# Clearing two tiles on VectorE at the start, and twelve extra matmuls ahead of the first transposes

## The chip, the cores and the metric

The kernel runs on one core of a Trainium2 chip. The core has engines that each work through their own queue of instructions in order: TensorE (PE in the profile; its weight loads are listed as PEld), VectorE (DVE), ScalarE (ACT), GpSimd (POOL) and SyncE (SP), which here does nothing but issue transfers. The metric is the time of one execution on the device in microseconds; lower is better. Engines wait for each other by semaphores; the waits that appear in the profile are inferred from these.

## The reference

A forward pass of a small speech model and all its gradients, in bf16:

```python
h = gelu(conv3(x, w1))[:, ::2, :]          # B=2, T=16000, D=256
f = gelu(conv3(h, w2))[:, ::2, :]          # 4000 rows left per batch
fe = einsum("btd,de->bte", f, w_f)
ge = einsum("bud,de->bue", g, w_g)         # U=8 rows per batch
j = tanh(fe[:, :, None, :] + ge[:, None, :, :])
out = einsum("btud,dv->btuv", j, w_o)      # 2 x 4000 x 8 x 256
```

The kernel returns `out` and the gradients with respect to x, w1, w2, g, w_f, w_g and w_o for a given `grad_out`, eight outputs in all.

## The kernel before

The 8000 rows of f (both batches after each other) are cut into chunks: one of 256 rows, then chunks of 512, then a rest. For each chunk three stages follow each other, and the stages of neighbouring chunks overlap: `stage_a` (L542) computes the two convolutions with their gelu and gelu derivative, and fe as the tile FE; `stage_j` (L636) computes the joint tanh, the output, and the gradients that go back through the tanh; `stage_de` (L813) takes the gradient back through the convolutions.

`stage_j` goes through u in four pairs. For each pair ScalarE makes the tile JT (L654): tanh(FE + ge), with channels on the partitions and ge as a bias from the tile GE. The gradient of w_o needs the same values with rows on the partitions, JR. The first two chunks get JR from JT by transposes on TensorE into a PSUM tile `psb` (L681), which VectorE or ScalarE copies out. All later chunks (except the last) compute it anew: VectorE adds FER, the rows of fe, and GEB, and ScalarE takes the tanh (L686, L691).

GEB is ge for one batch, spread over all 128 partitions: 8 x 256 values in every partition. `make_geb` (L606) makes it from GER, ge as rows: it clears the whole tile (L609), copies the ge rows into partitions 0, 32, 64 and 96 with four transfers issued by POOL, and, much later, spreads these within each 32 partitions by a VectorE shuffle (L615). Two such tiles are made, one for each batch. `ge_rows` (L626) computes GER with matmuls on gT and WG (transposed g and the weight w_g); `make_ge` (L1071) computes gT and GE.

The order of the instructions on each engine is not the order of the program text. Every piece of work is an operation with an engine, an estimated cost, its dependencies and a due time (`F.now` or `at`). `Flow.issue` (L107) simulates the engines with these estimates: it always takes the operation that can start first, then the one with the earlier due time, and emits it. What comes out is a fixed order for each engine's queue. Due times count in rows of f: 0 is the start of the first chunk's `stage_j`; `BIG` is -1e9 and so comes first. Dependencies given to an operation only steer this simulation; a real wait is set by the framework below where instructions touch the same tile.

The buffers come from classes with fixed numbers of slots. The class `ps` has seven PSUM banks, given to whichever operation needs one next; `geb` has two slots, one for each GEB tile.

Before the first chunk there is a head: VectorE clears a small tile (L1043), TensorE does twenty matmuls on it that nobody reads (`warm_up`, L1048), ScalarE does a first activation, POOL makes the identity, and the loads of x, the weights and g go out on the queues of SP, ACT and POOL. `mm` (L336) is the helper of nearly all matmuls, so that most of them carry its line, L337. `dma` (L357) is the helper of all transfers.

Of the kernel before, what the change touches and what calls it, by code (L numbers as in the profile page):

```python
# [10 lines left out]
BF16 = mybir.dt.bfloat16  # L11
# [25 lines left out]
class Flow:  # L37
# [24 lines left out]
    def buf(self, cls, shape, dtype, name):  # L62
        b = Buf(cls, shape, dtype, name)
        s = self.seq[cls]
        b.seq, s[0] = s[0], s[0] + 1
        return b

    def op(self, eng, cost, fn, r=(), w=(), new=(), at=None, work=0.0, after=(), kind=None, behind=(), sub=None, lag=0.0):
        o = Op()
        o.eng = (eng,) if isinstance(eng, str) else tuple(eng)  # L70
        o.cost = cost if isinstance(cost, tuple) else (cost,) * len(o.eng)
        o.fn, o.new, o.work, o.n = fn, list(new), work, len(self.ops)
        o.prio = ((self.now if at is None else at) + self.shift.get((self.stage, sub), 0.0), o.n)
        o.succ, o.done, o.ready, o.kind, o.span, o.lag = [], None, 0.0, kind, None, lag
        deps, bufs = set(after), []
        for lst, wr in ((r, False), (w, True)):
            for x in lst:
                b, key = x if isinstance(x, tuple) else (x, None)
                for d, k, dw in b.log:
                    if (wr or dw) and (k is None or key is None or k == key):  # L80
                        deps.add(d)
                if b not in bufs:
                    bufs.append(b)
        for lst, wr in ((r, False), (w, True)):
            for x in lst:
                b, key = x if isinstance(x, tuple) else (x, None)
                if wr:
                    b.log = [e for e in b.log if not (key is None or e[1] == key)]
                b.log.append((o, key, wr))
        for b in o.new:  # L90
            b.born = o
        deps.discard(o)
        o.soft = ({b.born for b in bufs if b.born is not None} | set(behind)) - deps - {o}
        deps |= o.soft
        for b in o.new:
            if b not in bufs:
                bufs.append(b)
        o.deps, o.bufs = deps, bufs
        for b in bufs:
            b.users += 1  # L100
        o.left = len(deps)
        for d in deps:
            d.succ.append(o)
        self.ops.append(o)
        return o
# [102 lines left out]
def c_pe(ns):  # L208
    return sum(max(n / 2.4 + 2.5, 25.0) for n in ns)
# [6 lines left out]
def c_dve(n, f=1.0):  # L216
    return 66.0 + 1.042 * n * f
# [3 lines left out]
def kernel(  # L221
# [19 lines left out]
    nc = tc.nc  # L241
    B, T, D = x.shape
    KK = w1.shape[0]
    U = g.shape[1]
# [6 lines left out]
    P = 128  # L251
# [42 lines left out]
    F = Flow(ctx, tc)  # L294
    op, buf = F.op, F.buf
# [9 lines left out]
    def fixed(shape, dtype, name, pool=None):  # L305
        b = Buf(None, shape, dtype, name)
        b.t = (pool or const).tile(shape, dtype, name=name)
        return b

    def psum(dt=FP32):  # L310
        return buf("ps", [P, CW if dt == FP32 else 2 * CW], dt, "ps" if dt == FP32 else "psb")
# [5 lines left out]
    WG = fixed([P, KT, D], BF16, "WG")  # L317
# [5 lines left out]
    GER = fixed([U, B, D], BF16, "GER")  # L323
# [6 lines left out]
    GE = fixed([P, B, KT, U], FP32, "GE")  # L330
# [5 lines left out]
    def mm(ps_ap, lhsT, rhs, start, stop):  # L336
        nc.tensor.matmul(ps_ap, lhsT=lhsT, rhs=rhs, start=start, stop=stop)  # L337
# [19 lines left out]
    def dma(q, out, in_, r, w, bytes_, new=(), transpose=False, at=None, after=(), cost=None, behind=(), sub="dma"):  # L357
        def go(e):
            eng_ = nc.sync if e == "SP" else nc.gpsimd if e == "POOL" else nc.scalar
            if transpose:  # L360
                eng_.dma_start_transpose(out=out(), in_=in_())
            else:
                eng_.dma_start(out=out(), in_=in_())
        c = cost or (1230.0 if transpose else 750.0 if q == "POOL" else 450.0)
        return op(q, c, go, r=r, w=w, new=new, at=at, after=after, behind=behind, sub=sub, kind="T" if transpose else "D",
                  work=bytes_ / 32768 * 165.0 if transpose else bytes_ / 304.0)
# [74 lines left out]
    def load_got(k, up, at):  # L441
        c = chunks[k]
        A, Pw = c.A, c.Pw
        GO = st[k]["GO"][up]
        GOT = buf("got", [P, NB, 2, KT, P], BF16, "GOT")
        if c.last:
            dma("SP", lambda: GOT[:].rearrange("p a u k c -> p (a u k) c")[:, 0:UP * KT, 0:2 * Pw],
                lambda: GO[:2 * Pw].rearrange("p a u v -> p (a u v)")[:, 0:UP * V], r=[GO], w=[GOT],
                bytes_=Pw * U * V * 2, new=[GOT], transpose=True, at=at)
            st[k]["GOT"] = {up: GOT for up in range(UP)}  # L450
            return
        dma("SP", lambda: GOT[:, 0:A, :, :, :Pw].rearrange("p a u k c -> p (a u k) c"),
            lambda: GO[:Pw, 0:A].rearrange("p a u v -> p (a u v)"), r=[GO], w=[GOT],
            bytes_=Pw * A * 1024, new=[GOT], transpose=True, at=at, sub="got")
        st[k].setdefault("GOT", {})[up] = GOT
# [149 lines left out]

    def make_geb(b):  # L606

        GEB = buf("geb", [P, U, D], BF16, "GEB")
        op("POOL", 2100.0, lambda e: nc.gpsimd.memset(GEB[:], 0.0), r=[(GER, b)], w=[GEB], new=[GEB])  # L609
        for q in range(0, P, 32):  # L610
            dma("POOL", lambda q=q: GEB[q:q + 1], lambda: GER[:, b, :], r=[(GER, b)], w=[(GEB, q)], bytes_=4096)

        def spread(e):
            v = GEB[:].rearrange("p u d -> p (u d)").bitcast(FP32)
            nc.vector.stream_shuffle(v, v, [0] * 32)  # L615
        op("DVE", 66.0 + c_dve(U * D // 2), spread, r=[GEB], w=[GEB], sub="geb", lag=45000.0 if b == 0 else 100000.0)
        return GEB

    def mix_geb(G0, G1):
        px = [c.px for c in chunks if c.px is not None][0]  # L620
        GEB = buf("gx", [P, U, D], BF16, "GEB")
        op("DVE", c_dve(U * D, 0.25), lambda e: nc.vector.tensor_copy(out=GEB[:], in_=G1[:]), r=[G1], w=[GEB], new=[GEB])
# [378 lines left out]
    def gg_out():  # L1001
# [43 lines left out]
       r=[(warm, 0)], w=[(warm, 1)])  # L1045
# [4 lines left out]
            mm(wps[:, 0:2 * P], warm[:, 0, 0], warm[:, 0].rearrange("p k c -> p (k c)"), True, True)  # L1050
    op("PE", 20 * 215.0, warm_up, r=[(warm, 0)], w=[wps], new=[wps])
    op("POOL", 500.0, lambda e: make_identity(nc, ident[:]), w=[ident])

    def wload(q, dst, out, in_, n, at, after=()):
        return dma(q, out, in_, r=[], w=[dst], bytes_=n * 65536, at=at, cost=450.0 if q != "POOL" else 550.0, after=after)
# [41 lines left out]
    def part(k):  # L1097
        return str(k) if k < 4 else "e" if k >= NG - 2 else "s"

    W0 = float(chunks[0].W)  # L1100
    stage_a(0, -W0, W0)
    F.now = -0.3 * W0
    make_ge()
    GEB = GEBX = None
    for k in range(NG + 1):
        c = chunks[min(k, NG - 1)]
        t0, Wk = (c.t0, float(c.W)) if k < NG else (float(NP), 300.0)
        if k < NG:
            F.stage = part(k)
            for up in range(1 if c.last else UP):  # L1110
                load_go(k, up, t0 + Wk * (up / UP - 0.7), [xh] if k == 0 else [])
                load_got(k, up, t0 + Wk * (up / UP - 0.5))
        F.stage = part(k)
        if k + 1 < NG:
            load_xc(k + 1, t0 - Wk * 0.3, [st[0]["GOT"][1].log[0][0]] if k == 0 else [])
        if k == 0:
            fr = st[1]["XCl"]
            wt(WFT, w_f[:, :], 1, W0 * 0.6, [fr])
            wt(W2T, w2.rearrange("i k n -> (i k) n"), KK, W0 * 0.7, [fr])
            wt(W1T, w1.rearrange("i k n -> (i k) n"), KK, W0 * 0.8, [fr])  # L1120
        if k + 1 < NG and chunks[k + 1].px is not None:
            F.now = t0 + Wk * 0.3
            GEB1 = make_geb(1)
            GEBX = mix_geb(GEB, GEB1)
        if k == 1:
            F.now = t0 + Wk * 0.1
            ge_rows()
            GEB = make_geb(0)
        if k < NG:
            F.stage = "j" + part(k)  # L1130
            stage_j(k, t0, Wk, GEBX if c.px is not None else GEB)
        if k < NG and c.px is not None:
            GEB = GEB1
        if k + 1 < NG:
            F.stage = "a" + part(k)
            stage_a(k + 1, t0, Wk)
        if k >= 1:
            F.stage = "d" + part(k)
            stage_de(k - 1, t0, Wk)
        F.stage = None  # L1140
        if k == NG - 1:
            F.now = t0 + Wk
            gg_out()
# [33 lines left out]
```

## Time and profile before

| | |
|---|---|
| runs, us | 789.6, 791.91, 789.79 |
| median, us | 789.79 |
| profiled execution, us | 789.48 |
| its span, first to last instruction, us | 787.7 |
| mean granted TensorE clock | 0.995 of full speed |
| two POOL clears of GEB | 11.88 to 15.42 us |
| first tanh of JT | 17.33 us |
| first transposes of JT | 17.88 us |
| second chunk's first convolution | 28.95 us |
| shuffles of GEB | 78.7 and 147.5 us |

All positions are microseconds from the start of the span. The page of the profile lists each engine's busy time and share of the span, then the span in 40 slices with the busy share of each in tenths, and the clock that TensorE was granted. The timeline lists instructions in order of their start, equal ones merged: start, length, engine, line, operation, tiles, shape, count, and in brackets how long the engine had been idle before and what ended that. The windows list, for a stretch, each engine's busy time and count of instructions, then the granted clock, the share of transfer engines in use, and GB/s. In groups "128x512 bf16" is partitions by elements.

### The profile page before, as it was taken

The numbers are of one execution on the slowest core, as the hardware profiler recorded it, in microseconds if no ns is written. First come the engines' busy times: TensorE is split into PE (matmuls) and PEld (weight loads), VectorE is DVE, ScalarE is ACT, GpSimd is POOL, SyncE is SP. The second block draws the span as 40 slices with busy tenths as digits, with TensorE's granted clock in tenths as the row PEclk, the third lists the DMA queues.
The fourth block names the chain that finished last, engine by engine and source line by source line (L and its number), as shares of the span: only waits on it lengthen the run. The fifth ranks groups of instructions, "written<-read, shape, count | busy, mean of one in ns | idle before, by whom it ended". The sixth has DMA issues, their size and how long they took to land. (4 is left out here: it accounts for less than half of the span.)

```text
span 787.7 us, 15636 instructions
## 1 busy us (share of the span) xinstructions
PE 770.0 (98%) x5668; PEld 533.6 (68%) x5668; DVE 714.1 (91%) x1503; ACT 725.5 (92%) x1178; POOL 96.2 (12%) x235
## 2 busy tenths in 40 slices
PE   6999999999999999999999999999999999999997
PEld 4657767576675767767677666676767767577775
DVE  5799999998998989989899898998989899899965
ACT  4999989999999999999999999999999999999833
POOL 4311110201102010020101101010020110203010
PEclk8999999999999999999999999999999999999999
DMA  9998999999999999999999999999998989989984
GB/s 212 175 208 187 232 252 244 238 240 243 222 227 227 266 232 215 233 257 225 229 211 244 243 230 226 214 257 219 229 252 203 264 209 227 248 225 239 229 204 144
DMA packets 382754, 178.86 MB, mean 227 GB/s; under 512 B 307762, under 2 KB 376468, under 8 KB 380756
## 3 DMA queue, kind: packets, MB, share of 16 engines
q1 hardware_dynamic: 381122, 176.90, 100.2%
q8 instruction: 44, 0.72, 0.4%
q10 hardware_dynamic: 1138, 0.66, 0.3%
q0 software_dynamic: 416, 0.30, 0.1%
q14 instruction: 34, 0.28, 0.1%
HBM read 51.42 MB, written 50.34 MB: 129 GB/s over the span
## 5 line engine op out<-in xcount | busy, mean ns | idle before, releaser
L654 ACT ACTIVATE JT<-FE,GE 128x512 bf16<-128x512 bf16 (+4 forms) x288 | 185.2, 691 | 0.1
L739 DVE SCALAR_TENSOR_TENSOR NGZ<-JSQ,ps 128x512 f32<-128x512 bf16 (+3 forms) x252 | 149.9, 608 | 3.5 <-PE ps L337 3.2
L337 PE MATMUL ps<-WO,JT 128*128 128x256 bf16 x1000 | 149.1, 273 | 0.0
L337 PE MATMUL ps<-GOT,WOT 128*128 128x512 bf16 (+2 forms) x544 | 147.2, 363 | 0.1
L346 ACT CAST OUT_SB<-ps 128x512 bf16<-128x512 f32 (+1 forms) x215 | 129.0, 604 | 11.8 <-PE ps L337 11.7
L337 PEld LDWEIGHTS <-JT 128*128 128x128 bf16 x1000 | 97.7, 98 | 54.7 <-issue 0.2
L726 ACT ACTIVATE JSQ<-JT 128x1024 bf16<-128x1024 bf16 (+2 forms) x129 | 130.0, 1008 | 4.5 <-DVE NGZ L739 4.2
L337 PE MATMUL GWO<-GO,JR 128*128 128x256 bf16 x1000 | 130.0, 273 | 1.5 <-ACT JR L691 0.8
L691 ACT ACTIVATE JR<-JR 128x1024 bf16<-128x1024 bf16 x112 | 120.3, 1076 | 8.4 <-DVE JR L686 8.1
L756 DVE TENSOR_TENSOR ZS<-ZS,NGZ 128x1024 f32<-128x1024 f32 (+2 forms) x102 | 115.3, 1131 | 0.4
L337 PEld LDWEIGHTS <-JR 128*128 128x128 bf16 x1000 | 97.5, 98 | 17.8 <-ACT JR L691 1.5
L520 DVE SCALAR_TENSOR_TENSOR g_s<-g_sq,ps 128x512 bf16<-128x512 bf16 (+2 forms) x102 | 64.8, 638 | 39.9 <-ACT HTo L517 31.4
L337 PEld LDWEIGHTS <-W 128*128 128x128 bf16 x612 | 57.9, 98 | 59.9 <-issue 2.8
L337 PE MATMUL ps<-XC,W 128*128 128x512 bf16 (+2 forms) x408 | 84.5, 362 | 1.4 <-DMA XC<-in_x_dram 1.4
L337 PEld LDWEIGHTS <-X 128*128 128x128 bf16 (+1 forms) x756 | 73.8, 98 | 9.6
L686 DVE TENSOR_TENSOR JR<-FER,GEB 128x1024 bf16<-128x1024 bf16 x112 | 77.6, 697 | 1.5 <-PE GWO L337 1.0
L809 DVE TENSOR_TENSOR ACC<-ACC,ps 128x512 f32<-128x512 f32 x90 | 59.1, 679 | 18.1 <-PE ps L337 18.1
L337 PEld LDWEIGHTS <-WOT 128*128 128x128 bf16 x544 | 51.7, 98 | 21.6 <-issue 0.9
L348 ACT ACTIVATE GX_SB<-ps 128x512 bf16<-128x512 f32 (+1 forms) x107 | 63.3, 619 | 2.1 <-PE ps L337 1.8
L379 POOL COPY GF<-GF 128x254 bf16<-128x254 bf16 (+1 forms) x17 | 7.4, 435 | 469.4 <-issue 313.6
L514 ACT ACTIVATE g_sq<-ps 128x512 bf16<-128x512 f32 (+2 forms) x102 | 60.7, 595 | 1.0 <-PE ps L337 0.6
L337 PE MATMUL ps<-W1T,GHo 128*128 128x512 bf16 (+1 forms) x252 | 61.3, 326 | 0.0
(144 smaller groups left out, 1171.3 us busy)
## 6 DMA issues: line engine op xcount, KB each, us to landing
GO<-in_grad_out_dram SPq DMA_DIRECT2D x60, 512.0 KB, 5.5
out_dram<-OUT_SB SPq DMA_DIRECT2D x60, 512.0 KB, 6.7
X<-in_x_dram SPq DMA_DIRECT2D x15, 1088.0 KB, 7.1
out_dram<-GX_SB SPq DMA_DIRECT2D x30, 512.0 KB, 3.5
GOT<-GO SPq DMA_TRANSPOSE x65, 5.0
GO<-in_grad_out_dram SPq DMA_DIRECT2D x4, 256.0 KB, 4.8
out_dram<-OUT_SB SPq DMA_DIRECT2D x4, 256.0 KB, 3.6
XC<-in_x_dram SPq DMA_TRANSPOSE x62, 4.9
```

Source lines behind the costliest of these rows:

```text
L337: nc.tensor.matmul(ps_ap, lhsT=lhsT, rhs=rhs, start=start, stop=stop)
L346: nc.scalar.copy(out=dst(), in_=src())
L348: nc.scalar.activation(out=dst(), in_=src(), func=ACT.Copy, scale=scale)
L514: op("ACT", c_act(W, True), lambda e, mt=mt, ps=ps: nc.scalar.activation(out=sq[:, 0:A, mt, :Pw], in_=fl(ps[:, :W], A), func=ACT.Square, s ...
L520: op("DVE", c_dve(W), lambda e, mt=mt, ps=ps: nc.vector.scalar_tensor_tensor(out=s[:, 0:A, mt, :Pw], in0=sq[:, 0:A, mt, :Pw], scalar=1.0, ...
L654: nc.scalar.activation(out=fl(jtw(JT, j)[:, mt], A)[:, :, lo:hi], in_=FE[:, 0:A, mt, lo:hi], func=ACT.Tanh, bias=GE[:, b, mt, 2 * up + j:2 ...
L686: op("DVE", c_dve(n * 2 * D, 0.5), lambda e, lo=lo, n=n, m=m, JR=JR: nc.vector.tensor_tensor(out=JR[:m, 0:n], in0=S["FER"][:m, lo:lo + n]. ...
L691: op("ACT", c_act(n * 2 * D), lambda e, n=n, m=m, JR=JR: nc.scalar.activation(out=JR[:m, 0:n], in_=JR[:m, 0:n], func=ACT.Tanh), r=[JR], w= ...
L726: nc.scalar.activation(out=JSQ[:, :, :W], in_=jtw(JT, j), func=ACT.Square)
L739: nc.vector.scalar_tensor_tensor(out=fl(zap(), A)[:, :, lo:hi], in0=fl(JSQ[:, d2, :W], A)[:, :, lo:hi], scalar=1.0, in1=fl(ps[:, :W], A)[: ...
L756: nc.vector.tensor_tensor(out=a, in0=a, in1=b, op=ALU.add)
L809: op("DVE", c_dve(512), lambda e: nc.vector.tensor_tensor(out=acc_ap().rearrange("p k d -> p (k d)"), in0=acc_ap().rearrange("p k d -> p ( ...
```

## The change

Three edits. `make_geb` no longer allocates and clears its tile; it takes one of two tiles that are made beforehand. These two are allocated in the head and cleared there by VectorE, written as 32-bit words, at the earliest due time, behind the clear of the small tile. And after `make_ge`, with a due time shortly before the first chunk's `stage_j`, TensorE gets twelve matmuls on WG (128 x 128 weights, 256 columns) into a PSUM bank that nobody reads. In the planner they depend on the second GE copy; the instructions themselves read only WG.

```diff
@@ make_geb @@
     def make_geb(b):
 
-        GEB = buf("geb", [P, U, D], BF16, "GEB")
-        op("POOL", 2100.0, lambda e: nc.gpsimd.memset(GEB[:], 0.0), r=[(GER, b)], w=[GEB], new=[GEB])
+        GEB = GEB01[b]
         for q in range(0, P, 32):
             dma("POOL", lambda q=q: GEB[q:q + 1], lambda: GER[:, b, :], r=[(GER, b)], w=[(GEB, q)], bytes_=4096)
 
@@ the head @@
     op("PE", 20 * 215.0, warm_up, r=[(warm, 0)], w=[wps], new=[wps])
     op("POOL", 500.0, lambda e: make_identity(nc, ident[:]), w=[ident])
+    GEB01 = []
+    for b in range(B):
+        GZ = buf("geb", [P, U, D], BF16, "GEB")
+        op("DVE", 650.0, lambda e, GZ=GZ: nc.vector.memset(GZ[:].rearrange("p u d -> p (u d)").bitcast(mybir.dt.uint32), 0), w=[GZ], new=[GZ])
+        GEB01.append(GZ)
 
@@ ahead of the loop over chunks @@
     F.now = -0.3 * W0
     make_ge()
     GEB = GEBX = None
+    if 12:
+        F.now = -0.05 * W0
+        fps = psum()
+
+        def fill(e):
+            for _ in range(12):
+                mm(fps[:, 0:D], WG[:, 0, 0:P], WG[:, 0], True, True)
+        op("PE", c_pe([D] * 12), fill, r=[WG, (GE, 1)], w=[fps], new=[fps])
     for k in range(NG + 1):
```

## The prediction

> **What bounds the kernel now.** I read the page's busy shares and its 40 slices first, then the granted clock in short windows, then the timeline of the first 30 us, and last the landing of the second chunk's input.
>
> ```profile
> PE 770.0 (98%) x5668; PEld 533.6 (68%) x5668; DVE 714.1 (91%) x1503; ACT 725.5 (92%) x1178; POOL 96.2 (12%) x235
> PE   6999999999999999999999999999999999999997
> PEclk8999999999999999999999999999999999999999
> ```
>
> TensorE is busy for 770.0 of 787.7 us. From 100 to 700 us the windows show 598.8 of 600, so there nothing but TensorE's own work sets the pace: time that is lost or won in the head is carried to the end. The only weak slice is the first, both in busy time and in clock. Everything that the change touches lies there. The timeline of before, 11 to 24 us:
>
> ```profile
> 11.88 3.54 POOL L609 MEMSET GEB<- 128x2048 bf16 x2
> 12.11 3.46 DVE L537 TENSOR_SCALAR g_s<-g_s 128x512 bf16<-128x512 bf16 x1
> 15.49 0.27 DVE L535 TENSOR_SCALAR g_sq<-g_sq 128x512 bf16<-128x512 bf16 x1
> ...
> 16.15 1.25 PE L337 MATMUL ps<-WG,gT 128*8 128x256 bf16 x4 [2.60 <-DVE g_s L520]
> ...
> 16.80 0.63 ACT L529 ACTIVATE g_s<-g_s 128x512 bf16<-128x512 bf16 x1 [3.36 <-DVE g_s L520]
> ...
> 17.33 2.09 ACT L654 ACTIVATE JT<-FE,GE 128x256 bf16<-128x256 bf16 x5
> ...
> 17.88 1.91 PE L681 MATMUL psb<-ident,JT 128*128 128x128 bf16 x8 [0.48 <-ACT JT L654]
> ...
> 20.68 0.58 ACT L346 CAST OUT_SB<-ps 128x512 bf16<-128x512 f32 x1 [0.34 <-PE ps L337]
> ...
> 22.09 0.59 ACT L346 CAST OUT_SB<-ps 128x512 bf16<-128x512 f32 x1 [0.41 <-PE ps L337]
> ```
>
> Columns: start, length, engine, line, operation, idle time before it and what ended it. The two GpSimd clears run from 11.88 to 15.42. The VectorE TENSOR_SCALAR that starts at 12.11 ends at 15.57, 0.15 us after them; the same shape takes 0.28 us at 10.35 and at 17.71. Everything in VectorE's queue behind it is late: L520 holds up TensorE (2.60 us) and ScalarE (3.36 us). TensorE had been idle from 13.54, and its clock fell. The windows around its fall and its return (the third number from the end of a line is the granted clock):
>
> ```profile
> 14.00:14.50 0.50, 0.00 (x0) 0.00 (x0) 0.50 (x1) 0.00 (x0) 0.50 (x1) 1.00 0.86 163
> 14.50:15.00 0.50, 0.00 (x0) 0.00 (x0) 0.50 (x1) 0.00 (x0) 0.50 (x1) 0.78 1.11 217
> 15.00:15.50 0.50, 0.00 (x0) 0.00 (x0) 0.50 (x2) 0.00 (x0) 0.43 (x1) 0.50 1.09 198
> ...
> 21.00:21.50 0.50, 0.50 (x4) 0.32 (x3) 0.39 (x2) 0.50 (x2) 0.50 (x2) 0.50 0.97 69
> 21.50:22.00 0.50, 0.50 (x6) 0.45 (x5) 0.47 (x4) 0.17 (x1) 0.50 (x2) 0.89 4.18 97
> ```
>
> It is halved from about 14.8 (0.78 as the mean of that half microsecond) to about 21.6: 6.8 us.
>
> **The change, part by part.**
>
> *The two POOL clears go.* With them goes the stall. An unhindered TENSOR_SCALAR of this shape is followed after 0.20 us (17.71 to 17.92); here the next one started after 3.38 (12.11 to 15.49). So VectorE runs 3.18 us earlier. What is late next: the second L520 would start at 13.18 and needs L514 (12.47 + 0.40 = 12.87); the FE cast at 13.59 needs its matmuls (12.64 + 0.60 = 13.24); the second GE copy at 14.25 needs matmuls that end at 13.54. None of these moves the 3.18. ScalarE's L529 goes from 16.80 to 13.62 and its first JT from 17.33 to 14.15. POOL itself: behind the clears stand only the row copies into GEB, which wait for GER (19.47 + 0.41); they go with VectorE to about 16.7, eight at 0.52 end by 21, before the second chunk's input lands at 24.3, and nobody reads GEB before the shuffle at 78.7.
>
> *The same two tiles are cleared by VectorE first thing.* No row of before has this fill. The nearest of its kind is the 128x128 uint32 clear, 0.165 us; eight times the words make 1.32 us at most. A VectorE copy of the same bytes (128x2048 bf16) takes 0.68. Two fills cost 1.36 to 2.64 us; I take 2.64, the row of the same kind. They stand behind the clear of g_sq (0.83 + 0.17), so the warm-up matmuls don't wait, and end by 3.64. VectorE was idle from 1.0 to 8.03: cost nothing, with 4.4 us of cover to spare; without that cover it would be 2.64.
>
> [...]
>
> *The twelve matmuls.* In TensorE's warm rows a 128x256 matmul takes 0.109 us (eight GWO from 21.89 to 22.76), in the cold stretch 0.215 (four from 19.58 to 20.44): 1.31 us, 2.58 at worst. They read only WG, landed by 12.3, and a PSUM buffer that an early GE copy frees at about 13.7; the wait for GE in their planned dependencies is no wait in the instruction. Ahead of them the four ge-row matmuls would run from 13.54 to about 13.9: their wait for L520 ends at 16.15 - 3.18 = 12.97 for the first pair, and for the second at 13.6. So the twelve run from 13.9 to 15.2. What they hold up are the eight JT transposes. These go by JT tiles: TensorE waits for the fourth until 19.07, now 15.89. Whatever ends before 15.89 costs nothing; by that the twelve have 0.7 us of room, and without it they would cost up to 1.31. By the planner's own costs they also fit: 12 x 109 = 1.31 us inside four tanh of 398 ns, so the order of all that follows should be the old one.
>
> *The clock.* With ge rows and the twelve there is no TensorE gap over 1.2 us (11.44 to 12.64) between 6.5 and 16. I take half of the 6.8 us as the period that decides. In the 3.4 us before the fall TensorE was busy 1.0 us (0.05 to 11.44, 0.9 from 12.64 to 13.54); now it would be 2.2, since it works on from 13.54. From 4.5 to 7.9, with a gap of 1.39, it was busy 2.0 us and the clock held. I take it as held. Then the transposes end at 16.17, and the next three groups of four (0.86, 0.85 and 0.60 at 19.58, 20.44 and 21.29) take 0.44 each: TensorE would be 4.4 us early. It cannot use all of that, since ScalarE is busy without a break from 22.57 to 28.01 and TensorE waits for its JR at 28.07. ScalarE wins the two waits of 0.34 and 0.41 that the slow matmuls cost: 3.18 + 0.75 = 3.93.
>
> [...]
>
> *What is late next.* The second chunk's first convolution starts at 28.95, now 25.02. Its input:
>
> ```profile
> L361 SPq DMA_TRANSPOSE XC<-in_x_dram x4: 1276/1302/1309, 14.4 to 18.5; - x4
> ...
> DMA to landing us min/median/max: 5.8/5.8/5.8
> ```
>
> The last transpose is issued at 18.5 and lands at 24.3. SP's queue up to there waits for nothing that moves (its waits end before 11 us), so 24.3 stays and 0.7 us of room is left. The first chunk's GOT lands at 15.0 (11.7 + 3.3) and is wanted at 16.6. Later SP issues that waited for GWO (29.14, 35.00) go with TensorE. From 28.95 to 50 VectorE is busy almost throughout, and starts from that convolution, so it moves as a whole.
>
> **Sum:** 3.18 + 0.75 + 0 + 0 = 3.93 us. The profiled execution took 789.48 us with a span of 787.7; 789.48 - 3.93 = 785.6. It stands 0.3 under the median of the runs shown (789.79), so a median may come out at 785.9; I give 785.7.
>
> **The rivals.**
>
> 1. *The clock falls all the same.* Where its periods lie against the program's start I can't see in one execution; 1.0 us busy was too little, 2.0 enough, and the border lies between. Then only the stall goes: 3.18, 786.3. Were the twelve cold to the last, they would end at 16.5 and push the transposes by 0.7: 787.0.
> 2. *The gain is partly given back in the second chunk.* The input has 0.7 us of room by one landing; the POOL copies of XC (0.65 at 24.71 where 0.19 was usual) and VectorE will meet in other places. Price: up to the 1.8 us that TensorE idles between 40 and 50 us, which is 787.4.
> 3. *The VectorE fills hold up POOL* until 3.64: the identity (1.01) and the two GR loads, which end at 2.65 and land 4.6 after issue, are up to 2.4 late. The GR transposes at 7.89 would wait about 1.7 us, between the two first convolutions: 787.3. For it, the stall that the trace shows the other way round; against it, that the earlier 0.165 us clear delayed nobody.
> 4. *The clears were not what held VectorE.* Then the twelve stand in the cold stretch behind 17.4 and end at about 20.0, 0.9 after the fourth tile: up to 1.0 later, 789.5 to 790.5. Against it: the ends at 15.42 and 15.57.
> 5. *Slower: the second chunk's input comes late.* The eight row copies of GEB now run at 16.7 to 21, beside its four transposes; each of them takes 4.4 us to land. If the input lands at 28.6 instead of 24.3, TensorE waits 3.6 us there and the clock falls; a halved stretch like the 6.8 us shown costs 3.4 more: 785.6 + 3.6 + 3.4 = 792.6. Slower from a landing of about 28.5 on. Against it: six of the eight already ran at 19.8 to 22.9 beside the same queue.
>
> **How the numbers follow.** Forecast 0.66, rivals in order 0.13, 0.09, 0.04, 0.04, 0.04. The range reaches from 784.5 (TensorE's 4.4 us, and a bit over half a microsecond between executions) to 787.6, which takes in rivals 1 to 3. About 0.3% (2.4 us) is what a measurement of this kernel can tell from no change, so faster means under 787.4: forecast, the first rival, and most of the second and third, 0.87; the same 0.09; slower 0.04.
>
> **What would show it.** Right: no VectorE TENSOR_SCALAR over 0.5 us before 16 us; the first JT at about 14.2; no clock below 1.00 between 12 and 22 us; the twelve ended before the fourth JT tile; the second chunk's convolution at about 25.0; TensorE's busy time lower by about 0.4 us (four groups of four go from 1.25, 1.06, 1.06 and 0.76 to 0.60, which is 1.73 less, and the twelve are 1.31 more). Wrong: a new wait for XC at the convolution, a clock of 0.50 somewhere before 50 us, GR transposes later than 7.9, or an order behind 30 us that is no longer the old one.

## The result

The changed kernel takes 786.91 us (median of 7 runs, 785.92 to 788.48), the kernel before 789.79 (7 runs, 789.43 to 792.01). The ratio is 0.9954, 95% interval 0.9941 to 0.9967: a gain of 0.33 to 0.59%. The forecast was 785.7 with a range of 784.5 to 787.6; the median lies in the range, 1.2 us above the forecast.

The profiled execution of the changed kernel took 787.74 us with a span of 786.0. Its page:

```profile
PE 769.5 (98%) x5649; PEld 534.5 (68%) x5680; DVE 711.4 (91%) x1503; ACT 726.3 (92%) x1180; POOL 93.7 (12%) x233
PE   7999999999999999999999999999999999999996
PEclk9999999999999999999999999999999999999999
```

In the first slice the clock has gone from 8 to 9 tenths and TensorE's busy share from 6 to 7. TensorE's busy time can't be compared to a tenth of a microsecond: 31 of its 5680 matmul records are missing here (weight loads are complete). The timeline of the changed kernel (start, length, engine, line, operation, idle time before it):

```profile
1.17 0.91 DVE L1055 MEMSET GEB<- 128x1024 uint32 x1 [0.16 <-issue]
1.49 1.16 POOL L363 DMA_DIRECT2D GR<-in_g_dram  x2 [0.18 <-issue]
2.24 0.91 DVE L1055 MEMSET GEB<- 128x1024 uint32 x1 [0.16 <-issue]
...
6.83 2.72 PE L337 MATMUL ps<-XC,W 128*128 128x256 bf16 x12 [1.32 <-DMA XC<-in_x_dram]
...
11.07 0.60 PE L337 MATMUL ps<-HTo,W 128*128 128x256 bf16 x4
...
13.79 0.28 DVE L537 TENSOR_SCALAR g_s<-g_s 128x512 bf16<-128x512 bf16 x1
13.99 0.28 DVE L535 TENSOR_SCALAR g_sq<-g_sq 128x512 bf16<-128x512 bf16 x1
...
15.69 1.49 PE L337 MATMUL ps<-WG 128*128 128x256 bf16 x12
15.84 2.09 ACT L653 ACTIVATE JT<-FE,GE 128x256 bf16<-128x256 bf16 x5
...
17.58 0.45 PE L680 MATMUL psb<-ident,JT 128*128 128x128 bf16 x5 [0.17 <-ACT JT L653]
...
18.75 0.56 ACT L346 CAST OUT_SB<-ps 128x512 bf16<-128x512 f32 x1
...
19.62 0.57 ACT L346 CAST OUT_SB<-ps 128x512 bf16<-128x512 f32 x1
...
25.58 0.40 POOL L407 COPY XC<-XC 128x254 bf16<-128x254 bf16 x1 [3.44 <-DMA XC<-in_x_dram]
```

The stall is gone: L537 takes 0.28 us instead of 3.46. The twelve matmuls end at 17.18, before the fourth JT tile releases the last transposes at 17.58. The two ScalarE copies at 18.75 and 19.62 no longer wait for TensorE. The clock stays up through the whole head (third number from the end):

```profile
14.00:16.00 2.00, 1.67 (x19) 1.31 (x19) 2.00 (x9) 1.62 (x6) 0.00 (x0) 1.00 0.70 134
16.00:18.00 2.00, 1.83 (x21) 1.50 (x20) 2.00 (x10) 2.00 (x6) 0.00 (x1) 1.00 0.92 180
18.00:20.00 2.00, 2.00 (x21) 1.80 (x19) 1.89 (x8) 2.00 (x5) 2.00 (x4) 1.00 1.06 94
```

But this execution is 1.68 us late by 11 us already: the convolution on HTo starts at 11.07, in the profile of before at 9.39. Its first twelve convolution matmuls took 2.72 us; those of before took 1.47, from 6.49. That is the pace of a halved clock (such matmuls came every 0.215 us at a granted 0.50 in the profile of before), although the granted clock reads 1.00 here and TensorE's queue up to there is the same. This pace makes 1.25 of the 1.68 us; another 0.34 comes from the input, which landed later in this execution (first matmul on it at 6.83 instead of 6.49). So I compare two stretches that leave the start out:

| profile | first convolution on HTo | second chunk's first convolution | D, between the two | last group of four full GHeR matmuls | E, from the second chunk on | span |
|---|---|---|---|---|---|---|
| before | 9.39 | 28.95 | 19.56 | 775.97 | 747.02 | 787.7 |
| changed | 11.07 | 26.43 | 15.36 | 773.95 | 747.52 | 786.0 |

All in microseconds. D fell by 4.20. The way from 787.7 to 786.0 is then: 4.20 won in the head, 1.68 lost at the very start of this execution, 0.50 given back behind the head (E), and 0.3 more from TensorE's last matmul to the end (782.52 to 787.7 before, 780.50 to 786.0 now). The sum is -1.7. That last stretch is 5.4 to 5.6 us long in the eight profiles of this document in which VectorE clears both tiles whole, and 5.1 to 5.2 in the six others; why was not looked into.

### The profile page after: what moved, and what is told of

Its sections match the earlier page's. It is cut to its first block, busy times and chain, and to the rows that moved or that the text cites. A ratio compares the mean times of both kernels' runs of the same rounds, so it can differ in the third digit from the quotient of the medians.

```text
span 786.0 us, 15627 instructions
## 1 busy us (share of the span) xinstructions
PE 769.5 (98%) x5649; PEld 534.5 (68%) x5680; DVE 711.4 (91%) x1503; ACT 726.3 (92%) x1180; POOL 93.7 (12%) x233
## 5 line engine op out<-in xcount | busy, mean ns | idle before, releaser
L346 ACT CAST OUT_SB<-ps 128x512 bf16<-128x512 f32 (+1 forms) x219 | 131.0, 603 | 9.6 <-PE ps L337 9.5
L337 PEld LDWEIGHTS <-WOT 128*128 128x128 bf16 x544 | 51.4, 98 | 21.6 <-issue 0.9
L348 ACT ACTIVATE GX_SB<-ps 128x512 bf16<-128x512 f32 (+1 forms) x104 | 61.6, 620 | 2.1 <-PE ps L337 1.8
L337 PE MATMUL ps<-GHoR,X 128*128 128x256 bf16 (+1 forms) x378 | 57.7, 273 | 0.0
```

What stands on the lines that cost most here:

```text
L346: nc.scalar.copy(out=dst(), in_=src())
L348: nc.scalar.activation(out=dst(), in_=src(), func=ACT.Copy, scale=scale)
```

## The experiments

Each is told by D and E as in the table, since single executions differ by the start and by the clock.

**The changed kernel again.** No edit.

> The changed kernel again, to see how its executions spread. I use one measure that leaves the very start out: D, from the first convolution on HTo to the start of the second chunk's first convolution (before: 9.39 to 28.95, 19.56 us; changed: 11.07 to 26.43, 15.36 us). Theory (the start has two modes, whatever the kernel: the clock is either up or still halved when the first input lands): D 15.36 again, the first twelve matmuls take either 1.5 or 2.7 us, and the times of both kernels fall into two groups about 1.6 us apart, before 789.6 and 791.5, this one 786.0 and 787.5. Rival (the change itself makes the first convolutions slow): they take 2.7 us here too and always, and before shows one group.

Median 786.6 us (6 runs), ratio 0.9953 (0.9940 to 0.9965). D is 15.36 once more, E 747.58. Its profile again has the slow start: the first twelve matmuls take 2.72 us. The times of before, taken beside it, run from 789.25 to 792.11 (29 runs), without a clean cut between two groups: 15 lie up to 790.24 and 14 from 790.72 on. So the late executions are not the change's alone. But the cause of each is not the same: six of before's 14 have a mean granted clock of 0.991 to 0.993 instead of 0.995, so their clock fell for longer, and that is not the slow start, which the granted clock does not show: in the changed kernel it reads 1.00 while the first twelve run at half the pace.

**Without the twelve matmuls.** `if 12:` becomes `if 0:`.

> The clears go to VectorE, the twelve matmuls are left out. Theory (the twelve keep the clock up): TensorE is busy only 1.5 of the 3.4 us before its old fall, the clock falls to 0.50 between 14 and 22 us, D is 16.1 to 16.4 (0.75 to 1.0 more than 15.36), time 0.8 to 1.0 us above the changed kernel. Rival (without the stall the gaps are too short, the clock stays up by itself and the twelve are idle work): no fall, D 15.36, time equal to the changed kernel within 0.3 us.

Windows of the kernel without the twelve (the clock is third from the end):

```profile
15.00:16.00 1.00, 0.59 (x7) 0.25 (x4) 1.00 (x6) 0.87 (x2) 0.00 (x0) 1.00 0.95 178
16.00:17.00 1.00, 0.46 (x2) 0.19 (x2) 1.00 (x5) 1.00 (x4) 0.00 (x0) 0.89 1.10 207
17.00:18.00 1.00, 0.88 (x7) 0.70 (x8) 1.00 (x5) 1.00 (x3) 0.17 (x1) 0.50 0.59 132
...
20.00:21.00 1.00, 1.00 (x10) 0.83 (x8) 0.72 (x3) 0.46 (x2) 1.00 (x3) 0.90 0.96 52
```

The clock falls before 17 and is back after 20, and D is 16.47: 1.11 more than with them, a little above what was expected. The median is 787.49 (12 runs), the ratio 0.9966 (0.9954 to 0.9977), which overlaps that of the changed kernel. In 2 of the 12 runs the mean clock was 0.999, so there it did not fall, and these are the shortest (786.13 and 786.22). The twelve thus take away a fall that comes in some executions and not in all. How often it comes isn't shown: the other ten runs have lower means (0.992 to 0.997), but such means also come with the twelve, from falls elsewhere.

**Only the twelve matmuls, the clears left on POOL.** The `fill` operation is added to the kernel before; every queue but TensorE's is unchanged.

> The two clears stay on POOL, only the twelve matmuls are added. Theory (the clears hold VectorE, the twelve then stand behind the ge-row matmuls in the cold stretch): VectorE's TENSOR_SCALAR still takes 3.4 us, the twelve take 2.6 us and end at about 20.0 with the start of before, D is 20.0 to 20.6, time 0.4 to 1.0 us above before. Rival (the twelve alone bring the gain, by the clock): D well under 19.5 and time 0.7 us or more below before.

The timeline of this kernel:

```profile
11.67 3.55 POOL L609 MEMSET GEB<- 128x2048 bf16 x2
11.89 3.46 DVE L537 TENSOR_SCALAR g_s<-g_s 128x512 bf16<-128x512 bf16 x1
...
17.12 2.74 PE L337 MATMUL ps<-WG 128*128 128x256 bf16 x12
```

Here the stall is what it was, and the twelve run at the pace of the halved clock, 2.74 us instead of 1.49 in the changed kernel. D is 19.83, 0.27 more than before, a bit less than expected. The median is 791.07 (12 runs), 0.83 above that of before beside it (790.24), but the ratio of 1.0003 (0.9994 to 1.0012) can't tell it from no change. Alone the twelve bring no gain.

**Half of each clear on POOL, half on VectorE.**

```diff
-  nc.vector.memset(GZ[:].rearrange(...).bitcast(mybir.dt.uint32), 0)
+  nc.vector.memset(GZ[:, 0:U // 2].rearrange(...).bitcast(mybir.dt.uint32), 0)
 ...
         GEB = GEB01[b]
+        op("POOL", 1050.0, lambda e: nc.gpsimd.memset(GEB[:, U // 2:U], 0.0), r=[(GER, b)], w=[GEB])
```

> Each tile is cleared half by VectorE at the start and half by POOL where it was before; the twelve stay. Theory (VectorE waits for the end of POOL's clears): two POOL clears of about 0.9 us, VectorE's TENSOR_SCALAR beside them takes 1.6 to 1.8 us instead of 3.46, D is 16.7 to 17.0. Rival (the stall comes from something else that left with the change): TENSOR_SCALAR 0.28 and D 15.36, or 3.4 and D near 18.5.

The timeline of the kernel with half clears on POOL:

```profile
13.39 1.84 POOL L609 MEMSET GEB<- 128x1024 bf16 x2
13.61 1.76 DVE L537 TENSOR_SCALAR g_s<-g_s 128x512 bf16<-128x512 bf16 x1
```

Half of the clear gives half of the stall: VectorE's instruction ends at 15.37, POOL's second clear at 15.23. With the whole, the half and the early clear (below) this settles that POOL's clears held VectorE. D was expected at 16.7 to 17.0 and is 17.76: the twelve came only at 16.97, after the clock had fallen, and took 2.74 us. The ratio is 0.9977 (0.9964 to 0.9990).

**28 instead of 20 unread matmuls at the start, on the changed kernel and on the one before.** `for _ in range(20)` becomes `range(28)`; the planned cost and so the order stay.

> The changed kernel with 28 instead of 20 unread matmuls at the very start, which bridge the pause before the first input (5.1 to 6.8 us). Theory (two modes of the start, by whether the clock rises in or after the warm-up; the slow one costs 1.6 us): the first twelve convolution matmuls take 1.5 us in the profile, the upper group of times (787.2 to 788.5) goes, median 785.9 to 786.4 and spread under 1.2 us. Rival (the VectorE fills at the start, or the later load of the input, make the first convolutions slow): they still take 2.7 us and the median stays at 786.6 to 787.0.

> The kernel before with 28 instead of 20 such matmuls, nothing else. Theory (the two modes are those of the start and not of this change): the upper group of before (790.7 to 792.1) goes, median 789.5 to 789.9. Rival (before's spread is another one): two groups and a median near 790.2 as before, or slower by the eight matmuls' 0.9 to 1.7 us.

In both profiles the first twelve convolution matmuls take 1.5 us (1.47 and 1.49), so the slow start is gone there. But the 28 end only at about 7.1, after the input has landed: the convolution on HTo starts at 9.87 and 9.94 instead of 9.39. The times are not as expected: 787.39 (6 runs, ratio 0.9957, 0.9944 to 0.9970) and 790.08 (12 runs, ratio 0.9996, 0.9986 to 1.0006). What else took the gain shows in the changed kernel with 28, in windows further on:

```profile
42.00:44.00 2.00, 1.04 (x15) 0.77 (x13) 2.00 (x7) 2.00 (x4) 0.58 (x2) 1.00 1.27 208
44.00:46.00 2.00, 1.76 (x12) 1.18 (x10) 2.00 (x8) 2.00 (x3) 0.00 (x0) 0.61 0.92 167
46.00:48.00 2.00, 2.00 (x8) 1.05 (x7) 2.00 (x6) 1.08 (x3) 0.00 (x0) 0.53 0.55 137
48.00:50.00 2.00, 2.00 (x11) 0.93 (x10) 0.90 (x4) 1.94 (x4) 0.00 (x0) 1.00 1.17 278
```

TensorE waits for VectorE until 41.8 and until 43.5 and is busy only 1.04 of 2 us; the clock falls for 3.4 us, and E grows to 749.38, 1.9 more than in the changed kernel. A low busy share alone doesn't explain that fall. The changed kernel has the same two waits (0.56 and 0.90 us), and there the clock held:

```profile
42.00:44.00 2.00, 1.19 (x11) 0.68 (x10) 2.00 (x6) 2.00 (x5) 0.97 (x3) 1.00 1.23 285
44.00:46.00 2.00, 1.05 (x12) 0.84 (x12) 2.00 (x6) 2.00 (x3) 0.44 (x1) 1.00 1.26 225
```

Over 3.4 us TensorE was busy for 1.65 us ahead of the fall (41.0 to 44.4) and 1.66 us in the changed kernel (42.14 to 45.54). Such a fall between 40 and 52 us shows in four of the profiles taken (this one, the twelve alone, the half clears, and the last one below). In the kernel before with 28, the fall of the head lies at 17.3 to 24.1 instead of 14.8 to 21.6, and D is 20.46. So where a fall lies, and whether it comes, differs between executions, and the theory of only two modes of the start was too simple.

**24 instead of twelve.** `range(12)` becomes `range(24)`, the planned cost as before.

> The changed kernel with 24 instead of twelve unread matmuls ahead of the transposes. Theory (twelve fit into the pause before the fourth JT tile with 0.6 us to spare; the rest is on the path): 24 take 2.6 us, end about 0.7 us after the fourth tile, D (first convolution on HTo to the second chunk's first convolution, 15.36 us in the changed kernel) 15.9 to 16.2, time 0.5 to 0.8 us above it. Rival (ScalarE, not TensorE, sets the pace up to 28 us, so there is more room than that): D 15.4 to 15.6, time the same within 0.3 us.

D is 16.04 (expected 15.9 to 16.2): 0.68 more for 1.31 us of matmuls. So, measured by D, the twelve had about 0.6 us of room. E is 747.54. The median is 787.43 (4 runs), ratio 0.9955 (0.9939 to 0.9972), too few and too spread to tell from the changed kernel's.

**The order of before kept.** The first chunks are planned as before, but the planner lets each GEB shuffle start a fixed lag after the copies into GEB, and these are now planned earlier. From the shuffles on (70 to 150 us) the order on TensorE, ScalarE, VectorE and POOL is another one. With longer lags the queues are again those of before, but for the edits themselves:

```diff
-  lag=45000.0 if b == 0 else 100000.0
+  lag=49399.0 if b == 0 else 105674.0
```

> The changed kernel, with the planner's lags of the two GEB shuffles set 4.4 and 5.7 us longer, so that they stand where they stood and every queue behind the head has the order of before. E is the time from the second chunk's first convolution to the last group of 4 GHeR matmuls but one on TensorE (before 28.95 to 775.97, 747.02 us; changed 26.43 to 773.95, 747.52). Theory (0.5 us of the gain was given back by the new order around the shuffles): E 747.0 to 747.15, time 0.4 to 0.5 us below the changed kernel. Rival (it is given back because the same transfers now meet other work, whatever the order): E 747.4 to 747.6, time the same.

E is 746.89, where the changed kernel had 747.52 and 747.58: the 0.5 us are back. The later profiles bear this out. Where the clock did not fall between 40 and 52 us, E is 747.00 to 747.13 in the three others with the longer lags, and 747.54 and 747.60 in the two others with the new order (24 matmuls, and none). In the changed kernel 0.28 of it goes between 130 and 145 us, beside the second shuffle (132.1 instead of 147.5); the first shuffle's move (72.0 instead of 78.7) costs nothing, and the rest goes little by little up to 700 us. D is 15.36, and the start of this execution is a quick one although VectorE clears its tiles there. The timeline's line for the second chunk's first convolution:

```profile
24.79 5.34 PE L337 MATMUL ps<-XC,W 128*128 128x512 bf16 x24
```

28.95 before, so 4.16 earlier, and the later convolutions keep that to the end. The median is 785.65 (6 runs), ratio 0.9942 (0.9930 to 0.9955).

**The same again, the clears early on POOL, and the same with 28.** Three kernels on one chip. For the second, VectorE does nothing at the start:

```diff
-  op("DVE", 650.0, lambda e, GZ=GZ: nc.vector.memset(...), w=[GZ], new=[GZ])
+  op("POOL", 2100.0, lambda e, GZ=GZ: nc.gpsimd.memset(GZ[:], 0.0), w=[GZ], new=[GZ], at=BIG)
```

> The changed kernel with the order of before kept (the longer lags), a second time, as the neighbour of the two kernels that follow. Theory: D 15.36, E 746.9 to 747.1 unless the clock falls again between 40 and 52 us, which costs 1.5; times in groups at 785.5 and 787.2, median 785.5 to 786.5. Rival (its first result was a lucky draw): median 786.6 or more.

> As the kernel with the kept order, but both clears are on POOL again, early: behind the two GR loads and ahead of the first copy of XC. Theory (what cost was the place of the clears beside VectorE's work, not the engine): POOL clears from about 2.7 to 6.2 us while VectorE is idle, the TENSOR_SCALAR takes 0.28, D 15.36, time equal to the kept order within 0.4 us. Rival (POOL is needed early: XC's copy at 6.5 or the WG load comes late): first convolutions or the matmuls on WG wait, 0.5 us or more slower.

> The kernel with the kept order and 28 instead of 20 unread matmuls at the start. Theory (the slow start goes, the later fall at 40 to 52 us stays): the first twelve convolution matmuls take 1.5 us, first convolution on HTo at 9.3 to 9.9, times 785.4 to 786.0 without the later fall and about 787.3 with it, median equal to the kept order or up to 0.5 lower. Rival (28 matmuls shift the later clock periods for the worse): median 0.5 or more above it.

The kept order gives 786.86 (6 runs, 785.53 to 787.16; ratio 0.9957, 0.9945 to 0.9969), D 15.36 and E 747.00. That is over the 786.6 that the rival named: its first median was a draw with few late executions, and what the kept order is worth rests on E, not on the medians. With 28 matmuls it is 786.54 (6 runs, 785.64 to 787.60; ratio 0.9957, 0.9945 to 0.9970), which can't be told from the same without them. The early clears on POOL give 785.29 (5 runs, 785.14 to 786.93), ratio 0.9943 (0.9931 to 0.9956), D 15.36, E 747.12. The median is 1.6 below the kept order's, not within 0.4 as expected; D and E agree with it, so what differs lies at the start and the end, if it isn't the draw of late executions (the intervals overlap). Their timeline:

```profile
2.64 3.57 POOL L1067 MEMSET GEB<- 128x2048 bf16 x2
6.49 0.40 POOL L407 COPY XC<-XC 128x254 bf16<-128x254 bf16 x1 [0.29 <-DMA XC<-in_x_dram]
...
12.11 0.28 DVE L537 TENSOR_SCALAR g_s<-g_s 128x512 bf16<-128x512 bf16 x1
12.31 0.28 DVE L535 TENSOR_SCALAR g_sq<-g_sq 128x512 bf16<-128x512 bf16 x1
```

The two instructions of 128x2048 are the same as before, on the same engine, and cost nothing: they end 0.3 us ahead of XC's copy. This execution starts as that of before did (9.39), which makes the pair the cleanest: L535 at 12.31 against 15.49, exactly the 3.18 of the forecast; the second chunk at 24.75 against 28.95, 4.20.

**The slow start without VectorE's clears.** The early clears on POOL once more.

> The early clears on POOL once more, for the slow start. An execution in which the clock never falls again after the start (mean granted clock 0.999 or 1.000) and which is still about 1.6 us longer than the shortest is one with the slow start: so it was in three profiled executions with the VectorE fills. Theory (the slow start comes by where the clock's periods lie, whatever runs on VectorE): some executions here are at 786.7 to 787.2 with such a clock, or the profile shows first convolution matmuls of 2.7 us, though VectorE does nothing at the start. Rival (the VectorE fills beside the warm-up make it): none of that; all with such a clock within 785.0 to 785.8, as in its first five.

The median is 786.09 (6 runs, 785.30 to 786.54), ratio 0.9941 (0.9927 to 0.9955). None of the 11 executions with the early POOL clears bears the mark of the slow start; of the 12 with the kept order and VectorE's clears, two do (787.12 and 787.20 with a clock of 1.0). That is what the rival says, but also what chance gives often enough with such numbers. The profiles lean the same way: of the seven with 20 matmuls at the start and VectorE's clears, five start slowly; of the four with 20 and none on VectorE, none does. The timeline of this execution shows the twenty matmuls at the slow pace to their end (4.45 us, 0.22 each) and no harm behind them (1.47 us for the twelve):

```profile
1.06 4.45 PE L337 MATMUL ps<-g_sq 128*128 128x256 bf16 x20 [1.06 <-DVE g_sq L1042]
6.57 1.47 PE L337 MATMUL ps<-XC,W 128*128 128x256 bf16 x12 [1.06 <-DMA XC<-in_x_dram]
```

By the pace of these matmuls the clock rose there in the pause between 5.5 and 6.6 us. The kept order's second profile, with VectorE's clears, does the same (4.45, then 1.47 from 6.31).

## Why the prediction was right, and where it was off

- *The stall.* Right to the hundredth: 3.18 us in the pair with equal starts. The fourth rival falls with it: the stall followed the clears when they were halved and when they were moved.
- *The fills on VectorE.* Each takes 0.91 us by its row, and 1.07 from start to start, where the forecast took 1.32; they end at 3.2, and VectorE's next work comes at 8.99 here (8.03 before). The GR loads are issued at 1.49 and take 1.16 as before, so POOL wasn't held up, and the third rival falls. The 1.07 us are 1024 words at 1.04 ns, and half clears of 512 words come 0.54 us apart.
- *The twelve matmuls.* Right: less the late start of 1.68, they start at 14.01 and the next instruction follows at 15.33 (forecast 13.9 to 15.2), and the fourth tile releases the transposes at 15.90 (15.89). The room of 0.7 us measured about 0.6 by D. The forecast's way to it had left out that three transposes come before the fourth tile (17.01 to 17.41), so on TensorE itself only a wait of 0.17 us is left; why D loses no more than 0.68 is not shown.
- *The clock.* Held, as forecast: in the head of all nine profiles with twelve or 24 matmuls and no clear beside VectorE's work, so the first rival did not come. Without the twelve it fell in the profile taken. The reason given, that 1.0 us busy in half of the 6.8 us is too little and 2.0 enough, is not what decides alone: 1.66 us was enough in the changed kernel, and 1.65 too little with 28. That half of the 6.8 us is a period that decides was an estimate: falls of 3.4 us were measured (below), but no run shows that busy time over such a period brings them. The clock's term was 0.75 and measured 1.02 (4.20 - 3.18): mis-sized, because I added up two idle times before ScalarE's copies. They are counted from the listed end of the instruction in front, and ScalarE starts its next about 0.1 us before that end (18.35 + 0.49 in front of 18.75). By starts the first copy came 0.43 us closer to the JT tile in front of it, and the second 0.54 us closer to the first.
- *The second chunk's input* was in time: copied by POOL from 25.58 on, the last copy ending at 26.22, and wanted at 26.43. The eight early row copies did not hold it up, so the fifth rival falls. That VectorE is busy almost throughout from 28.95 was misread (2.52 of 6 us from 28 to 34 in the profile of before); nothing came of it.
- *The order behind.* Wrong. The step that failed is "so the order of all that follows should be the old one". The twelve do fit into the planned pause, and up to the shuffles nothing moved. But a shuffle's planned start hangs on the planned end of the copies into GEB, and these moved. It cost 0.5 us, shown by E with the kept order. So the second rival's loss came, but around the second shuffle and not in the second chunk.
- *The start.* Not in the forecast at all, and neither were the 0.3 us at the end. The sum took the start of the profiled execution of before as given, and that was one of the quick ones. If the three shortest runs of the changed kernel are taken as quick ones (no profile shows their start), 789.5 became 785.9 to 786.3, which is the forecast with 0.5 given back. The median of before, 789.79, lies among its early executions, and that of the changed kernel, 786.91, does not; with such a spread (2.6 us) that is the luck of seven runs. The 786.91 are therefore not a sign of a weaker effect in the head, where D fell by 4.2.

What stays open: whether VectorE's clears beside the first matmuls make the slow start more frequent. They don't make it always (two profiles with them and 20 matmuls start quickly), and it has shown in no profile without them (five of seven against none of four). But before, which has no such clears, has eight late executions of 29 with a mean clock of 0.995 or 0.996, and no profile shows how those start. The number of executions doesn't decide it. Open too are what decides whether the clock falls between 40 and 52 us, and why the end is longer with VectorE's clears.

## What to carry to other kernels

Two clears on GpSimd, 11.88 to 15.42 us, stopped a TENSOR_SCALAR on VectorE here until 0.15 us after their end: it took 3.46 us instead of 0.28. Look for single instructions that take ten times their usual time, and for what ends with them; then move the long one to where the other engine is idle, which may be on its own engine. When a hand-planned order hangs on planned times, changing one operation's cost early can reorder a part far behind, and keeping the old order shows what that is worth. And where executions spread by more than the effect, measure the change on a stretch of the trace between two fixed instructions: D agreed within 0.02 us in eight profiles whose times lay up to 3.1 us apart.

## What the runs showed of the hardware

Two clears one behind the other kept VectorE out for both (3.46 us for two of 1.80 each, 1.76 for two halves of 0.95 each); it did not get in between them.

The granted clock stayed down for 6.8 us in before, for 3.4 without the twelve, and for 3.4 from 44 us on in the changed kernel with 28. TensorE had not been idle for that long: in before the clock fell 1.24 us into a gap of 2.6 us, and in the changed kernel with 28 after gaps of 0.56 and 0.82 with little work between them (1.04 of 2 us). Nor did it fall after every such pair: it held through gaps of 0.56 and 0.90 in the changed kernel. And the granted clock does not show the slow start of the changed kernel: it reads 1.00 while the first twelve matmuls take 2.72 us instead of 1.47. The same head started slowly in both profiles of the changed kernel (2.72 us) and quickly in both with the kept order (1.47); what decides that is not shown.
